# A four-layer attention and Fourier network on one core: head operands packed by halves of the sequence, output-weight pieces chained, stored weight parts loaded one by one

## The chip, the cores and the metric

The kernel runs on one core of a Trainium2 chip. The metric is the device time of one execution in microseconds (us). A core has TensorE (PE; its weight loads are listed as PEld), VectorE (DVE), ScalarE (ACT), GpSimd (POOL) and SyncE (SP), each working through its own list of instructions in order. They wait for each other through semaphores. In this kernel SP issues all transfers between device memory and the on-chip buffer (SBUF); matmul results land in eight banks of a small accumulator memory (PSUM).

## The reference, cut to what matters

The input `x` has 2048 rows (sequence, S) of 640 (D). Four layers follow each other, each with a layer norm before it and the input added after it: attention, Fourier, attention, Fourier, with the same weights both times.

```python
def _A_ref(x, wqkv, wo):
    H = 32; Dh = D // H; W = 256
    qkv = (x @ wqkv).reshape(B, S, 3, H, Dh).transpose(2, 0, 3, 1, 4)
    q, k, v = qkv[0], qkv[1], qkv[2]
    scores = einsum("bhqd,bhkd->bhqk", q, k) * (Dh ** -0.5)
    mask = (idx[:, None] - idx[None, :] >= 0) & (idx[:, None] - idx[None, :] < W)
    p = softmax(where(mask, scores, -1e9), axis=-1)
    o = einsum("bhqk,bhkd->bhqd", p, v)
    return o.transpose(0, 2, 1, 3).reshape(B, S, D) @ wo

def _B_ref(x, dft_seq_re, dft_seq_im, dft_hid_re, dft_hid_im):
    a = einsum("bsd,ed->bse", x, dft_hid_re)
    b = einsum("bsd,ed->bse", x, dft_hid_im)
    return einsum("ts,bse->bte", dft_seq_re, a) - einsum("ts,bse->bte", dft_seq_im, b)

x = x + _A_ref(_layernorm(x), A_wqkv, A_wo)
x = x + _B_ref(_layernorm(x), ...)
x = x + _A_ref(_layernorm(x), A_wqkv, A_wo)
x = x + _B_ref(_layernorm(x), ...)
```

The change touches the attention layers alone: 32 heads of 20 columns, and a window of 256 positions back.

## The kernel before, in words

**Number format.** Every operand of a large product is held as two parts, `hi` (the value rounded to the matmul's format by ACT) and `lo` (what is left, subtracted by DVE or POOL). A product is three matmuls: hi x hi, hi x lo, lo x hi. The output weights `wo`, 640 x 640, are cut into such parts once, in the first attention, and stored in device memory (`wod`) for both.

**The head loop (`heads`, L666).** Heads go in eight quads of four. A quad has 16 blocks of 128 query rows, so there are 128 steps, and `step` runs from -10 to 128. In one step three stages stand beside each other: the scores of block `s = step + 10` (`s_head`, L691), from which DVE takes each row's maximum (L696); the transposed scores of block `t = step` with the maximum subtracted (`t_pair`, L719), their exponentials on ACT (L729) and masks on POOL (L735, L739); and the product with the values of block `v = step - 1` (`pv`, L754), copied by ACT (L761), so that each step has one such copy. Every four blocks (one of the four 512-column blocks of the sequence, `sb`) the maxima are transposed on PE (L704), copied by ACT to `mt` (L707) and sent by SP as a row of the quad's q operand (`qp<-mt`, L709); the transposed scores need that row some four steps after. Every four blocks too, `finish` (L765) sends sums and results out (`sm<-ou`, `o_d<-ou`, `r_d<-rc`), with DVE's reciprocal of the sums between them.

**Operands of a quad (`pack`, L642).** The q and k columns, computed as chunks of 128 rows and stored by 512-column blocks (`qk_d<-c`, 512 KB), are loaded into one of two buffer sets, by quad number odd or even. For each 512-column block there are 12 loads of 20 rows x 2 x 512. The list `due` (L789) says when: for quad q and block j at `s = 16q + 4j - 8`, so a block every four steps; `defer(i // 3, f)` (L862) puts three loads in each of four steps. If a chunk's block isn't yet stored (`packable`), `pack` first runs its pending jobs (`flush`) and advances the slots until it is. Quad 0 is packed before the loop.

**Filling.** Between these stages `fill` gives PE other work, in order: the projections of the later q and k chunks (`project`, L618; L275), then the first three fifths of the output product (`partials`, L1040), then the rest (`late`).

**Slots, lanes, posts.** `tick` (L191) is the clock of the schedule: two slots a step. `post(d, f)` runs `f` d slots later. The lanes "act" and "pool" are queues of small jobs of which each tick emits one. All of this is decided when the program is built; at run time there are only the lists of the engines.

**Pieces of `wo` (`keep_wo`, L548), first attention only.** Ten pieces of 128 x 320: load `rr<-wo` (L557), 5 slots later a cut job (ACT writes `hi`, L237; POOL writes `lo` in two halves of 160 columns, L229), 2 slots later two stores `wo_d<-rr` (L561). A piece starts every six steps, at steps 2, 8, ... 56; at step 62 the three buffers `rr` return to their other use.

**Output product.** `prepare(2)` (L1008), when the projections have two block pairs left, loads the parts of the first three fifths of `wo` (`load_wo`, L1022: two loads of 320 KB for each fifth) and asks for the attention results. The asks wait in `self.asks`; a tick pops one (L196) when three raw buffers of five are free in turn. An ask loads results (`x<-o_d`) and reciprocals (`rr<-r_d`), has POOL scale them and ACT and POOL cut them. `poll_late` (L1097) loads the other two fifths near the end of the loop.

The lines in which the order of the work around the change is set:

```python
                for i, f in enumerate(self.pack(q, j)):
                    defer(i // 3, f)
        if self.asks and self.room(3):
            self.asks.popleft()()
        self.post(5, lambda: self.cut_job("pool", ("wo", i), hi, lo, raw, lambda: self.post(2, keep)))
```

Of the kernel before, what the change touches and what calls it, by code (L numbers as in the profile page):

```python
# [7 lines left out]
F32 = mybir.dt.float32  # L8
# [7 lines left out]
P = 128  # L16
# [51 lines left out]
class Net:  # L68
    def __init__(self, nc, tc, ctx, a):
# [26 lines left out]
        self.od = dram.tile([H, 32, S], F32, name="o_d")  # L96
        self.wod = dram.tile([2, KC, P, D], F32, name="wo_d")
        self.wqd = dram.tile([NCH, P, 2 * D], F32, name="wq_d")
# [92 lines left out]
    def tick(self):  # L191
        self.slot += 1
        for k in sorted(k for k in self.posted if k <= self.slot):
            for f in self.posted.pop(k):
                f()
        if self.asks and self.room(3):  # L196
            self.asks.popleft()()
        for lane in self.lanes.values():
            for _ in range(2 if self.lead else 1):
                if lane and lane[0][0] <= self.slot:  # L200
                    lane.popleft()[2]()
# [18 lines left out]
    def sub_job(self, lane, key, lo, src, hi, done=None):  # L220

        eng = {"dve": self.nc.vector, "pool": self.nc.gpsimd}[lane]
        n = 2 if lane == "pool" and len(src.shape) == 2 else 1
        w = src.shape[-1] // n
# [323 lines left out]
    def keep_wo(self, i):  # L548

        if i == 0:  # L550
            self.wt = [self.slot_tile(f"rr{n}", 512, dt)[:, :320] for n, dt in enumerate((F32R, F32R, F32))]
        if i == 2 * KC:
            self.rr = [self.slot_tile(f"rr{n}", 512, F32) for n in range(3)]
            return
        k, cs = i // 2, slice(i % 2 * 320, i % 2 * 320 + 320)
# [3 lines left out]
        def keep():  # L559
            for n, t in enumerate((hi, lo)):  # L560
                self.nc.sync.dma_start(self.wod[n, k, :, cs], t.bitcast(F32))  # L561
        self.post(5, lambda: self.cut_job("pool", ("wo", i), hi, lo, raw, lambda: self.post(2, keep)))

# [77 lines left out]

    def pack(self, quad, sb):  # L642

        todo = []
        cols = slice(sb * 512, (sb + 1) * 512)
        for c in range(160 * quad // P, -(-160 * (quad + 1) // P)):
            while self.slot is not None and c > 1 and (c, sb) not in self.packable:
                self.flush(("qk", c, sb))
                if self.heavy:
                    self.relieve()  # L650
                self.tick()
# [14 lines left out]
    def heads(self, xsrc, xdst, hook):  # L666
# [120 lines left out]
        for c, u in [(c, u) for c in range(NCH - 2) for u in range(2)] + [(c, sbs[0] // 2) for c, sbs in LAST]:  # L787
            pos[c, u] = 2 * per_piece * (len(pos) + 1)
        due = [(16 * q + 4 * j - AHEAD, pos[-(-160 * (q + 1) // P) - 1, j // 2])  # L789
               for q in range(1, NQ) for j in range(NSB)]  # L790
        self.xsrc = xsrc
# [50 lines left out]
        for step in range(-LEAD, steps + 1):  # L842
# [8 lines left out]
            for f in later.pop(step, []):  # L851
                f()
            if self.fresh and step >= 0 and step % 6 == 2 and step // 6 <= 2 * KC:
                self.keep_wo(step // 6)
            s, t, v = step + LEAD, step, step - 1
            if due and s >= due[0][0]:
                while done[0] < due[0][1]:
                    fill(15)
                due.pop(0)
                q, j = (s + AHEAD) // 16, (s + AHEAD) % 16 // 4  # L860
                for i, f in enumerate(self.pack(q, j)):
                    defer(i // 3, f)  # L862
# [141 lines left out]
    def prepare(self, n):  # L1004
# [3 lines left out]
        if n == 2:  # L1008
# [5 lines left out]
            for k in ks:  # L1014
                self.load_wo(k, self.early_w[k])
            self.ask(0)
# [5 lines left out]
    def load_wo(self, k, w):  # L1022
        for n in range(2):
            self.nc.sync.dma_start(w[n].bitcast(F32), self.wod[n, k])

# [41 lines left out]
    def ready_part(self):  # L1067
        t = self.part_t
        return t == NB or t % 4 or not (self.early_o[t // 4 % 2]["left"])

# [20 lines left out]
    def poll_late(self, n):  # L1091

        if n == 1:
            self.late_w = pairs(cuts(self.qp[0][:, :4 * D], D))
            self.late_c = [self.work.tile([P, 1024], F32, name="cr", tag="c", bufs=3) for _ in range(3)]
            for k in range(EARLY, KC):
                self.load_wo(k, self.late_w[k - EARLY])  # L1097
        if n in (1, 4):
# [801 lines left out]
```

## Time and profile before

| What | us |
|---|---|
| Median of 3 runs (2223.17 to 2227.18) | 2225.28 |
| Time of the profiled execution | 2228.1 |
| Span of the profiled execution, first to last instruction | 2226.4 |
| First head loop, first to last output copy of L761 | 164.7 to 556.6 |
| Second head loop, first to last output copy of L761 | 1274.9 to 1654.4 |

The page shows one profiled execution. Its first part gives the busy time of each engine and its share of the span, then the number of instructions. In views of waits, a row reads "engine, what it was about to do, what ended the wait: us in total, times, longest". In timelines, a row is "start, length, engine, line, operation, output <- inputs (shape) and how many were merged; in brackets the idle time before and what ended it". SPq rows are issues of transfers, whose length is the issue alone; "DMA" rows in the chain of waits run from issue to landing. PE's granted clock is given as a share of full speed.

### The profile page before, as it was taken

Reading aid. Unit: us, or ns where it says so; the run is one execution under the profiler, and the core shown is the slowest. Engines: PE = TensorE matmul, PEld = TensorE weight load, DVE = VectorE, ACT = ScalarE, POOL = GpSimd, SP = SyncE. Lnnn points to the kernel's source line nnn. Section 1 sums busy time; section 2 is a strip of 40 time slices with the busy share of each in tenths; the row PEclk is TensorE's granted clock in tenths of the full one; section 3 lists DMA queues with packets and bytes.
Section 4 is the critical chain, followed back from the end, with each engine's and each line's share of the span. In section 5 each row is a group of like instructions: output and inputs, shape, how many; then the busy total and the mean of one; then the engine's idle time right before and its main releaser. Section 6 shows DMA issues by size and latency. Waiting matters only on the chain.

```text
span 2226.4 us, 48984 instructions
## 1 busy us (share of the span) xinstructions
PE 2127.7 (96%) x17944; PEld 1791.7 (80%) x17944; DVE 1597.3 (72%) x3910; ACT 1115.6 (50%) x2080; POOL 999.4 (45%) x1648
## 2 busy tenths in 40 slices
PE   7999989899989999999999999989889999999999
PEld 7987767677768888889999877767777788888898
DVE  7358777675898768786661578867758978687766
ACT  2127766556554545452441277666565545455332
POOL 3048767776514132332330377668655132331324
PEclk9999999999999999999999999999999999999999
DMA  6556776775635454656645566676844354546653
GB/s 219 176 187 213 219 238 210 209 225 162 195 118 172 137 169 136 224 178 205 207 160 181 170 206 197 215 215 206 233 153 152 117 183 140 173 138 219 218 172 119
DMA packets 227728, 410.14 MB, mean 184 GB/s; under 512 B 40352, under 2 KB 90784, under 8 KB 227488
## 3 DMA queue, kind: packets, MB, share of 16 engines
q1 hardware_dynamic: 227488, 407.01, 57.6%
q8 instruction: 142, 2.33, 0.5%
q14 instruction: 98, 0.80, 0.1%
HBM read 282.13 MB, written 123.60 MB: 182 GB/s over the span
## 4 chain that ended last, share of the span: by engine, by line
PE 76%; DVE 7%; DMA 6%; POOL 3%; ACT 3%; issue 3%; SPq 2%; ACTq 0%; DVEq 0%; POOLq 0%
PE banks L1449 29%; PE banks L257 15%; PE banks L275 12%; PE banks L754 6%; PE banks L719 5%; PE banks L1738 4%; PE banks L691 4%; ACT pt L729 1%; DMA qp<-mt 1%; DMA qp<-qk_d 1%; DVE banks L696 1%; DMA x<-o_d 1%; DMA kp<-qk_d 1%; DVE qp L250 1%; DVE big L1062 1%
## 5 line engine op out<-in xcount | busy, mean ns | idle before, releaser
L696 DVE CUSTOM_DVE_ANT_0 banks<-banks,mask 128x384 f32<-128x384 f32 (+2 forms) x1024 | 528.1, 557 | 164.2 <-PE banks L691 140.1
L729 ACT ACTIVATE pt<-banks 128x768 f32<-128x768 f32 (+2 forms) x512 | 394.2, 771 | 199.0 <-PE banks L719 85.9
L735 POOL TENSOR_SCALAR_AFFINE_SELECT pt<-pt 128x256 f32<-128x256 f32 x512 | 208.9, 408 | 211.4 <-ACT pt L729 194.9
L275 PE MATMUL banks<-big,wc 64*128 64x512 f32 x1920 | 273.3, 397 | 0.4 <-DVE pt L461 0.4
L719 PE MATMUL banks<-qp,kp 61*128 61x384 f32 (+2 forms) x1024 | 210.3, 382 | 33.4 <-DMA qp<-mt 16.5
L691 PE MATMUL banks<-kp,qp 60*128 60x384 f32 (+2 forms) x1024 | 205.8, 345 | 14.3 <-ACT pt L729 10.1
L754 PE MATMUL banks<-pt,vq 128*32 128x128 f32 x5760 | 213.4, 279 | 5.1 <-POOL pt L735 2.8
L275 PEld LDWEIGHTS banks<-big,wc 64*128 64x128 f32 x1920 | 189.5, 187 | 21.9 <-ACT x L594 1.9
L754 PEld LDWEIGHTS banks<-pt,vq 128*32 128x32 f32 x5760 | 143.0, 110 | 55.5 <-issue 37.2
L719 PEld LDWEIGHTS banks<-qp,kp 61*128 61x128 f32 x1024 | 108.6, 185 | 96.4 <-DVE mc L696 56.1
L739 POOL TENSOR_SCALAR_AFFINE_SELECT pt<-pt 128x256 f32<-128x256 f32 x448 | 182.4, 407 | 0.0
L244 ACT ACTIVATE qp<-pt 128x512 fp32r<-128x512 f32 (+1 forms) x195 | 119.8, 624 | 112.9 <-DVE pt L1383 53.5
L244 ACT ACTIVATE c<-pt 128x512 fp32r<-128x512 f32 x150 | 93.6, 626 | 159.1 <-POOL pt L1369 53.0
L250 DVE TENSOR_TENSOR c<-pt,c 128x512 fp32r<-128x512 f32 x150 | 124.1, 828 | 55.5 <-ACT c L244 52.9
L250 DVE TENSOR_TENSOR qp<-pt,qp 128x512 fp32r<-128x512 f32 (+1 forms) x191 | 155.1, 819 | 12.2 <-ACT qp L244 9.5
L1449 PE MATMUL banks<-qp,big 128*128 128x512 f32 x630 | 156.3, 401 | 4.3 <-ACT qp L244 1.8
L1382 POOL TENSOR_TENSOR pt<-pt,pt 128x512 f32<-128x512 f32 x34 | 50.7, 1491 | 239.3 <-DMA pt<-c 153.7
L691 PEld LDWEIGHTS banks<-kp,qp 60*128 60x128 f32 x1024 | 125.2, 188 | 34.7 <-ACT pt L729 13.9
L1449 PEld LDWEIGHTS banks<-qp,big 128*128 128x128 f32 x630 | 121.4, 194 | 31.1 <-ACT qp L244 2.7
L696 DVE DVE_READ_ACCUMULATOR2_ANT mc<- 128x1 f32 x1024 | 145.2, 142 | 0.0
L1449 PE MATMUL banks<-qp,xc 128*128 128x512 f32 x480 | 117.2, 390 | 0.7 <-DVE xc L250 0.7
L1449 PEld LDWEIGHTS banks<-qp,xc 128*128 128x128 f32 x480 | 89.9, 188 | 20.2 <-DVE xc L250 1.6
(242 smaller groups left out, 4442.0 us busy)
## 6 DMA issues: line engine op xcount, KB each, us to landing
pt<-c SPq DMA_DIRECT2D x188, 512.0 KB
qk_d<-c SPq DMA_DIRECT2D x80, 512.0 KB
kp<-qk_d SPq DMA_DIRECT2D x384, 80.0 KB
qp<-qk_d SPq DMA_DIRECT2D x384, 80.0 KB
kp<-u_d SPq DMA_DIRECT2D x32, 640.0 KB
o_d<-ou SPq DMA_DIRECT2D x64, 256.0 KB
x_d<-x SPq DMA_DIRECT2D x48, 320.0 KB
v_d<-pt SPq DMA_DIRECT2D x16, 768.0 KB
```

The lines of the kernel that those rows point to most:

```text
L244: nc.scalar.activation(hi, src, AF.Copy, scale=-1.0 if neg else 1.0)
L250: (eng or nc.vector).tensor_tensor(out=lo, in0=src, in1=hi.bitcast(F32), op=OP.subtract)
L257: self.nc.tensor.matmul(p, x, y, start=n == 0, stop=n == last)
L275: self.nc.tensor.matmul(ps[a], x[r], y[r], start=half + i == 0, stop=half == 1 and i == n - 1, skip_group_check=True)
L691: nc.tensor.matmul(p, qp[quad % 2][b:b + 60, z, qb * P:(qb + 1) * P], kp[quad % 2][b:b + 60, z, k0 * P:(qb + 1) * P], start=True, stop=True)
L696: nc.vector.tensor_tensor_reduce(out=p, in0=p, in1=self.mask[:, 384 - n * P:], scale=1.0, scalar=NEG, op0=OP.add, op1=OP.max, accum_out=mc ...
L719: nc.tensor.matmul(self.banks[:, banks[e], :n * P], kp[quad % 2][b:b + 61, z, kb * P:(kb + 1) * P], qp[quad % 2][b:b + 61, z, kb * P:(kb + ...
L729: nc.scalar.activation(pt[quad, kb][:, 2 * z:2 * z + 2, :n * P], self.banks[:, b0:b1 + 1, :n * P], AF.Exp, scale=SCALE)
L735: nc.gpsimd.affine_select(out=t[:, :, 0:P], in_=t[:, :, 0:P], pattern=[[0, 2], [1, P]], compare_op=OP.is_ge, fill=0.0, base=0, channel_mul ...
L739: nc.gpsimd.affine_select(out=t[:, :, 256:384], in_=t[:, :, 256:384], pattern=[[0, 2], [-1, P]], compare_op=OP.is_gt, fill=0.0, base=0, ch ...
L754: nc.tensor.matmul(self.banks[32 * h:32 * h + 32, bank, :P], vq[:, 96 * (kb % 4) + 21 * h:96 * (kb % 4) + 21 * h + 32], t[:, h, (qb - kb) ...
L1449: nc.tensor.matmul(self.banks[:, bk, :], p, b[q], start=start and m == 0, stop=stop and last and m == 2, skip_group_check=True)
```

## The change

Four things are edited, in the attention alone.

- Quads 1 to 7 are packed by halves of the sequence: 12 loads of 20 rows x 2 x 1024 at `s = 16q - 8` for blocks 0 and 1, and 12 at `s = 16q` for blocks 2 and 3, again three a step. Both blocks of a half have to be stored by then.
- The pieces of `wo` form a chain: piece 0 starts at step -2, and each piece starts the next when its own stores are issued. The cut is posted 9 slots after the load (5 before). POOL subtracts a piece's 320 columns at once. The `rr` buffers return after the last piece.
- `wod` keeps both parts of a fifth side by side, so that one load of 640 KB brings them. At `prepare(2)` these loads are posted 5, 7 and 9 slots later.
- An ask is popped when two raw buffers are free in turn (three before).

```diff
-        self.wod = dram.tile([2, KC, P, D], F32, name="wo_d")
+        self.wod = dram.tile([KC, P, 2, D], F32, name="wo_d")
...
-        if self.asks and self.room(3):
+        if self.asks and self.room(2):
             self.asks.popleft()()
...
-        n = 2 if lane == "pool" and len(src.shape) == 2 else 1
+        n = 2 if lane == "pool" and len(src.shape) == 2 and src.shape[1] > 320 else 1
...
         if i == 0:
             self.wt = [self.slot_tile(f"rr{n}", 512, dt)[:, :320] for n, dt in enumerate((F32R, F32R, F32))]
-        if i == 2 * KC:
-            self.rr = [self.slot_tile(f"rr{n}", 512, F32) for n in range(3)]
-            return
         k, cs = i // 2, slice(i % 2 * 320, i % 2 * 320 + 320)
         hi, lo, raw = self.wt
         self.nc.sync.dma_start(raw, self.a["wo"][:, k, cs])
 
         def keep():
             for n, t in enumerate((hi, lo)):
-                self.nc.sync.dma_start(self.wod[n, k, :, cs], t.bitcast(F32))
-        self.post(5, lambda: self.cut_job("pool", ("wo", i), hi, lo, raw, lambda: self.post(2, keep)))
+                self.nc.sync.dma_start(self.wod[k, :, n, cs], t.bitcast(F32))
+            if i < 2 * KC - 1:
+                self.keep_wo(i + 1)
+            else:
+                self.rr = [self.slot_tile(f"rr{n}", 512, F32) for n in range(3)]
+        self.post(9, lambda: self.cut_job("pool", ("wo", i), hi, lo, raw, lambda: self.post(2, keep)))
...
-    def pack(self, quad, sb):
+    def pack(self, quad, sb, n=1):
 
         todo = []
-        cols = slice(sb * 512, (sb + 1) * 512)
-        for c in range(160 * quad // P, -(-160 * (quad + 1) // P)):
-            while self.slot is not None and c > 1 and (c, sb) not in self.packable:
-                self.flush(("qk", c, sb))
+        cols = slice(sb * 512, (sb + n) * 512)
+        for c, i in [(c, i) for c in range(160 * quad // P, -(-160 * (quad + 1) // P)) for i in range(sb, sb + n)]:
+            while self.slot is not None and c > 1 and (c, i) not in self.packable:
+                self.flush(("qk", c, i))
                 if self.heavy:
                     self.relieve()
                 self.tick()
...
-        due = [(16 * q + 4 * j - AHEAD, pos[-(-160 * (q + 1) // P) - 1, j // 2])
-               for q in range(1, NQ) for j in range(NSB)]
+        due = [(16 * q + 8 * j - AHEAD, pos[-(-160 * (q + 1) // P) - 1, j]) for q in range(1, NQ) for j in range(2)]
...
-            if self.fresh and step >= 0 and step % 6 == 2 and step // 6 <= 2 * KC:
-                self.keep_wo(step // 6)
+            if self.fresh and step == -2:
+                self.keep_wo(0)
...
-                q, j = (s + AHEAD) // 16, (s + AHEAD) % 16 // 4
-                for i, f in enumerate(self.pack(q, j)):
+                q, j = (s + AHEAD) // 16, (s + AHEAD) % 16 // 8
+                for i, f in enumerate(self.pack(q, 2 * j, 2)):
                     defer(i // 3, f)
...
             for k in ks:
-                self.load_wo(k, self.early_w[k])
+                self.post(5 + 2 * k, lambda k=k: self.load_wo(k, self.big[0][:, k * 2 * D:(k + 1) * 2 * D]))
...
     def load_wo(self, k, w):
-        for n in range(2):
-            self.nc.sync.dma_start(w[n].bitcast(F32), self.wod[n, k])
+        self.nc.sync.dma_start(w.bitcast(F32), self.wod[k].rearrange("p l c -> p (l c)"))
...
             for k in range(EARLY, KC):
-                self.load_wo(k, self.late_w[k - EARLY])
+                self.load_wo(k, self.qp[0][:, (k - EARLY) * 2 * D:(k - EARLY + 1) * 2 * D])
```

More of the change, by code (lines that the diff above doesn't have):

```diff
@@ L1068, in ready_part @@
         t = self.part_t
-        return t == NB or t % 4 or not (self.early_o[t // 4 % 2]["left"])
+        return t == NB or t % 4 or not self.early_o[t // 4 % 2]["left"]
     def late_set(self, sb):
```

## Prediction

> **What bounds the kernel now.** I read the page first, then the busy time by stretches, then the waits, then the queue's timeline where PE stood still. The page gives the span and shows TensorE busy nearly throughout, so only its few idle microseconds can be won.
>
> ```profile
> span 2226.4 us, 48984 instructions
> PE 2127.7 (96%) x17944; PEld 1791.7 (80%) x17944; DVE 1597.3 (72%) x3910; ACT 1115.6 (50%) x2080; POOL 999.4 (45%) x1648
> kp<-qk_d SPq DMA_DIRECT2D x384, 80.0 KB
> qk_d<-c SPq DMA_DIRECT2D x80, 512.0 KB
> big<-wo_d SPq DMA_DIRECT2D x12, 320.0 KB
> ```
>
> The change sits in the head loop, which runs twice, and the two passes differ in little but the weight work of the first (`fresh`). Three stretches of each, cut at the same steps (first, 76th and 91st output copy of L761, then the last), give the busy time; after the length come PE, PEld, DVE, ACT, POOL, granted clock, DMA share, GB/s.
>
> ```profile
> 164.70:381.90 217.20, 205.70 (x2879) 156.72 (x2880) 166.08 (x629) 152.89 (x285) 161.92 (x372) 0.98 0.70 218
> 381.90:434.50 52.60, 43.57 (x576) 32.33 (x577) 33.33 (x128) 31.03 (x57) 37.99 (x82) 0.90 0.78 230
> 434.50:556.60 122.10, 111.86 (x1724) 92.43 (x1720) 83.98 (x278) 73.41 (x135) 84.70 (x184) 1.00 0.65 191
> 1274.90:1477.90 203.00, 201.58 (x2879) 154.38 (x2880) 165.42 (x629) 146.63 (x266) 144.52 (x342) 1.00 0.66 203
> 1477.90:1529.30 51.40, 42.84 (x576) 32.01 (x577) 33.41 (x128) 30.99 (x57) 37.86 (x82) 0.93 0.81 230
> 1529.30:1654.40 125.10, 113.76 (x1724) 94.19 (x1720) 83.88 (x279) 73.42 (x136) 84.80 (x184) 0.97 0.63 188
> ```
>
> With the same 2879 matmuls the first stretch takes 217.2 us in the first pass and 203.0 in the second: 14.2 us are lost to the weight work. The second pass shows the undisturbed step: 203.0/75 = 2.71 us, 1.35 a slot. At that pace the 15 steps of the middle stretch are 40.6 us, so it loses about 12 and 11 us. The waits of the first pass and one place of ACT's and SP's timelines tell what the 14.2 are:
>
> ```profile
> ACT rr L237 <- DMA rr<-wo: 5.5, 4, 3.0
> ACT rr L237 <- DMA wo_d<-rr: 4.4, 1, 4.4
> 290.14 0.36 SPq L557 DMA_DIRECT2D rr<-wo  x1
> 294.34 0.47 ACT L237 ACTIVATE rr<-rr 128x320 fp32r<-128x320 f32 x1 [3.00 <-DMA rr<-wo]
> 332.23 0.69 PE L691 MATMUL banks<-kp,qp 60*128 60x384 f32 x1 [4.37 <-ACT pt L729]
> ```
>
> ACT reaches the weight cut before its load has landed and stands with all exponentials queued behind it; PE follows. The middle stretch of the second pass shows the other stall:
>
> ```profile
> 1477.24 2.79 SPq L1024 DMA_DIRECT2D big<-wo_d  x6
> ...
> 1481.84 0.51 SPq L944 DMA_DIRECT2D x<-o_d  x1
> 1482.90 1.87 SPq L654 DMA_DIRECT2D qp<-qk_d  x3
> 1485.44 0.61 SPq L771 DMA_DIRECT2D sm<-ou  x1
> 1486.82 0.34 SPq L772 DMA_DIRECT2D o_d<-ou  x1
> 1487.68 0.43 SPq L777 DMA_DIRECT2D r_d<-rc  x1
> 1489.07 0.37 SPq L573 DMA_DIRECT2D qk_d<-c  x1
> 1490.18 1.06 SPq L654 DMA_DIRECT2D kp<-qk_d  x3
> ...
> 1493.84 1.16 SPq L709 DMA_DIRECT2D qp<-mt  x2
> 1481.84 8.33 DMA x<-o_d
> 1493.84 4.04 DMA qp<-mt
> 1483.60 0.25 ACT L707 ACTIVATE mt<-banks 16x128 fp32r<-16x128 f32 x1
> 1492.09 0.44 PE L691 MATMUL banks<-kp,qp 60*128 60x384 f32 x2 [2.02 <-DVE mc L696]
> 1498.02 0.69 PE L719 MATMUL banks<-qp,kp 61*128 61x384 f32 x2 [5.13 <-DMA qp<-mt]
> ```
>
> All transfers go through SP in order. The load of 1481.84 lands at 1490.17, and the eighth transfer after it goes out at 1490.18: the queue holds eight, and the ninth waits for the oldest. Six weight loads of 320 KB fill it; the row maxima `mt`, ready at 1483.85, go out 10 us later, and PE stands 2.02 and 5.13 us.
>
> **The change part by part.**
>
> *Weight pieces chained, 14.2 us in play.* A piece now starts when the one before is stored, and its cut is posted 9 slots after the load, not 5: 4 x 1.35 = 5.4 us more, over the longest of both waits (3.0, 4.4). From piece store to the next write of `hi` there are ten slots, where the kernel before had four in the worst case. Walking the lanes, the ten pieces end about slot 166, six before `prepare(2)` at 172; no later wait takes the stall's place. POOL does one subtraction of 320 columns for two of 160:
>
> ```profile
> L229 POOL TENSOR_TENSOR rr<-rr,rr x20: 522/527/534, 181.4 to 334.2; 128x160 fp32r<-128x160 f32 x20
> L654 SPq DMA_DIRECT2D kp<-qk_d x384: 273/335/1427, 54.3 to 1592.2; - x192
> ```
>
> That is at most 0.5 us each, on an engine with room: nothing. Bounds of the part: 0 to -14.2; I take -12.7, leaving 1.5 for bursts (below).
>
> *Packing by halves.* Quads 1 to 7 take 24 loads of 160 KB for 48 of 80 KB: 168 issues fewer a pass, x 0.335 = 56 us of SP's time, in a loop of 380 us, and each of these issues also took one of the eight places in the queue. That is why the first pass's queue ran late (the 290.14 load above went out with a cut due at 291). But 12 loads of 160 KB now go in four steps and none in the next four: 1.92 MB in 4 x 2.71 = 10.8 us. With two qk stores of 512 KB, an o store and a v load (1.47 MB) this is 314 GB/s, where the row of the full queue below moved 265. 3.39/0.265 = 12.8 us, 2 us late at the end of the burst, and drained when the next `mt` goes out two slots later. What `mt` may lose shows where nothing is late:
>
> ```profile
> 1440.48 0.25 ACT L707 ACTIVATE mt<-banks 16x128 fp32r<-16x128 f32 x1
> 1447.84 0.44 PE L719 MATMUL banks<-qp,kp 61*128 61x384 f32 x2 [0.35 <-DVE mc L696]
> 1480.00:1500.00 20.00, 12.85 (x170) 9.81 (x163) 11.07 (x41) 8.75 (x18) 9.70 (x21) 0.88 0.91 265
> ```
>
> 7.1 us from copy to use, and a landing takes about 4. In the first pass a burst also meets a 640 KB weight store and 480 KB of pieces: 4.5 MB, 17 us, some 3.5 us late at `mt`: just at the limit. Bounds: 0 to +2 for each of five such bursts; I took 1.5 in all. Loads two blocks early overwrite nothing in use: the blocks of two quads before were last read by step 16(q-2)+7.
>
> *Weight loads spread, room(2).* At `prepare(2)` six loads become three of 640 KB, at 5, 7 and 9 slots. The o loads of block 0 come first, the third two slots earlier, and one of block 1 is let in. Up to the `mt` in question: o 1.28 MB, o of block 1 0.51, one weight load 0.64, qk store 0.51, sums and o store 0.26, three packs 0.48 = 3.69 MB; before, the same count is 4.46 MB and took from 1477.24 to 1497.88, 217 GB/s. Transfers grow from 0.186 to 0.217 MB on average, and with eight in the queue I scale to 254 GB/s: 1.3 + 14.5 us, `mt` at 15.8 to 16.3 against a need at 1483.85 + 7.1 = 13.7 after 1477.24. So 2.5 us late for 7.15 (2.02 + 5.13): -4.65. At 217 it would be 4.6 late, at 265 1.5.
>
> The half clock behind a long gap goes too: the row of 1480 to 1500 has 0.88. [...] Of the 10.8 us that the middle stretch of the second pass loses (51.4 - 40.6), 7.15 and, below, 1.36 are gaps; of the 2.3 left I put 1.5 to this clock: -6.15 a pass, -12.3 in all; bounds -8 to +2 a pass.
>
> *A wait that gets longer.* At step 86 the packing of quad 6 finds chunk 8 not yet stored: it empties the POOL lane ahead of the masks and holds SP until the store has landed. Now it needs blocks 2 and 3, not 2 alone, and the earlier o jobs stand ahead:
>
> ```profile
> 1512.01 1.44 POOL L229 TENSOR_TENSOR c<-x,c 128x256 fp32r<-128x256 f32 x2
> 1515.96 0.41 PE L754 MATMUL banks<-pt,vq 128*32 128x128 f32 x4 [0.37 <-POOL pt L735]
> 1517.37 0.41 PE L754 MATMUL banks<-pt,vq 128*32 128x128 f32 x4 [0.99 <-POOL pt L735]
> 469.04 0.45 PE L719 MATMUL banks<-qp,kp 61*128 61x384 f32 x2 [1.95 <-DMA qp<-mt]
> 1565.32 0.69 PE L719 MATMUL banks<-qp,kp 61*128 61x384 f32 x2 [3.98 <-DMA qp<-mt]
> ```
>
> PE stood 1.36 us. Two more subtractions of 0.72 each and one of an o job come ahead of the masks: +2 a pass (0 to +4), +4 in all. Behind POOL's masks wait the PV matmuls; behind SP's wait stand that step's `mt`, sums and v load, whose 7.1 us are then nearly used up. The additional o load has a second price here: it holds one of the five raw buffers, so the copy of (8, 3) runs the clock of slots on by two at step 83 until one is free, 1.4 us of POOL work sent ahead, on an engine busy 37.86 of 51.4 us; nothing to +1, within the +2.
>
> *The late quads.* The 3.98 us at 1565 (1.95 in the first pass) are again `mt` behind packs, in steps that now have none: -5 in all, clock included; bounds 0 to -8. The four loads at the tail (L1097) become two, not on the path.
>
> Sum: -12.7 - 12.3 + 4 - 5 = -26. The profiled execution took 2228.1 us (span 2226.4), 2.8 above the median 2225.28; 2228.1 - 26 = 2202.1, less 2.8 is 2199.
>
> **The rivals.**
>
> *Only the chain pays.* The middle stretch moves its bytes at 0.81 DMA share already, and the half-pack of quad 6 puts 0.96 MB more into the same steps. From slot 173 to 186 there fall due weights 1.97, o loads 1.79, packs 1.92, qk stores 1.02, o store and v 0.64: 7.3 MB in 18.9 us, 388 GB/s. If the lateness then only moves on to the next `mt`, four steps behind, the spread loads win nothing: -12.7 - 5 + 4 = -13.7, 2212 beside the median. Against it: the stall was one of order, six loads that nobody needed yet ahead of one that PE needed.
>
> *All stalls go.* 14.2 of the first stretch, 2 x 8.65 at `prepare(2)` (7.15 and the clock), 7.5 of the late quads (3.98 and 1.95, and the clock behind the longer), 2 x 1.36 at step 86: 41.7 us, 2184. For it: SP is relieved of 56 us of issues a pass. Against it: step 86 gets more to do, not less.
>
> *Slower: the bursts.* If a burst moves 2 us worse than I reckon, `mt` lands behind its 7.1 us after each one, 14 a pass. It decides from 3 us of lateness in the queue. At 1.5 us each, 28 x 1.5 = 42 less the 26 won: 2241. For it: 314 GB/s wanted, 265 seen when the queue was full. Against it: the first stretches moved 218 and 203 GB/s at shares of 0.70 and 0.66, which is 311 and 308 at full share; at that rate a burst is late by a tenth of a microsecond, and the four steps behind it want no pack at all.
>
> [...]
>
> *It doesn't do what it says.* Fewer issues, yet `mt` and the weight load stand behind the same bytes, since those do not change: 2225. Against it: the 5.4 us that the cut gains are written into the order and depend on no rate.
>
> **How the numbers follow.** Forecast 0.60 (own range 2189 to 2209), only the chain 0.14, all stalls 0.08, slower 0.13, nothing 0.05. Low 2185 to high 2221 leaves out the slower case and part of "all". A measurement here tells 0.2%, 4.5 us: faster 0.82, same 0.05, slower 0.13.
>
> **What would show it.** ACT no longer waits for `rr<-wo` or `wo_d<-rr`, and the first stretch of the first pass is near 204.5; `mt` at the 81st copy goes out within 6 us; three loads of 640 KB stand apart; PE's gaps at step 86 grow to about 3.4. Gaps of L719 for `mt` every eight steps would prove the slower case.

## The result, and the profile after

| Kernel | Median, us | Runs | Ratio to before, 95% interval |
|---|---|---|---|
| before | 2226.23 (2223.17 to 2227.95) | 4 | |
| after | 2260.59 (2254.01 to 2265.38) | 4 | 1.0154 [1.0122, 1.0186] |

The change makes the kernel 34 us slower, where 26 us of gain were forecast. The spans of the profiled executions lie 28.8 us apart. The page of the changed kernel, its span, its busy times and two of the issue rows:

```profile
span 2255.2 us, 48553 instructions
PE 2138.0 (95%) x17944; PEld 1791.5 (79%) x17944; DVE 1594.0 (71%) x3910; ACT 1117.9 (50%) x2080; POOL 1005.7 (45%) x1638
kp<-qk_d SPq DMA_DIRECT2D x168, 160.0 KB
big<-wo_d SPq DMA_DIRECT2D x6, 640.0 KB
```

The change did what it says: 168 loads of 160 KB for 336 of 80 KB in each of the two rows, the same 17944 matmuls. The lines of the head loop have moved by one (the scores are L692, the reciprocal L775, the exponentials L730). The same six stretches as before, cut at the same output copies, with the same columns:

```profile
167.10:389.20 222.10, 208.85 (x2879) 156.60 (x2880) 165.70 (x629) 153.18 (x285) 161.10 (x361) 0.97 0.74 214
389.20:450.60 61.40, 46.19 (x577) 33.88 (x577) 33.30 (x128) 32.34 (x60) 42.95 (x90) 0.86 0.74 198
450.60:577.00 126.40, 114.44 (x1722) 94.01 (x1719) 83.60 (x279) 73.01 (x134) 80.21 (x176) 0.97 0.63 179
1293.50:1496.30 202.80, 200.47 (x2879) 151.96 (x2878) 165.59 (x628) 146.82 (x265) 144.94 (x341) 1.00 0.73 205
1496.30:1557.70 61.40, 46.30 (x576) 33.87 (x577) 33.42 (x128) 32.07 (x59) 42.92 (x90) 0.86 0.73 198
1557.70:1684.50 126.80, 114.73 (x1724) 94.02 (x1720) 83.76 (x279) 73.20 (x134) 80.33 (x177) 0.97 0.65 179
```

Against before, the first stretch of the first pass has +4.9 where -12.7 was forecast; the two middle stretches +8.8 and +10.0; the late ones +4.3 and +1.7. The first stretch of the second pass is unchanged at 202.8, with the same packing but without the weight work of the first pass (the pieces of `wo`, and the cutting and storing of the other weights). So the loss needs either that work beside the packing or the work of the middle stretch.

What PE stands behind has changed too. The page's groups of instructions, each with its idle time and the largest releaser at the end; before, then after:

```profile
L719 PE MATMUL banks<-qp,kp 61*128 61x384 f32 (+2 forms) x1024 | 210.3, 382 | 33.4 <-DMA qp<-mt 16.5
L691 PE MATMUL banks<-kp,qp 60*128 60x384 f32 (+2 forms) x1024 | 205.8, 345 | 14.3 <-ACT pt L729 10.1
```

```profile
L720 PE MATMUL banks<-qp,kp 61*128 61x384 f32 (+2 forms) x1024 | 210.0, 386 | 25.9 <-DVE mc L697 14.1
L692 PE MATMUL banks<-kp,qp 60*128 60x384 f32 (+2 forms) x1024 | 200.2, 350 | 33.9 <-DVE mc L697 32.6
```

The waits for `mt` and for ACT no longer lead (in the first pass `mt` costs 3.6 us for 7.4), and the next scores wait 32.6 us for DVE's row maxima, for 4.1 us before. DVE has no more to do: 1594.0 us busy, for 1597.3. The waits of the first pass say what held it, first of before, then of after:

```profile
DVE rc L774 <- DMA sm<-ou: 4.9, 3, 2.6
```

```profile
DVE rc L775 <- DMA sm<-ou: 33.3, 12, 10.3
PEld banks L692 <- DVE mc L697: 30.5, 27, 7.6
PE banks L692 <- DVE mc L697: 23.1, 10, 7.2
PE banks L720 <- DMA qp<-mt: 3.6, 1, 3.6
```

The reciprocal of the sums (`rc`) stands in DVE's list nine slots after `finish`. In the place shown here `sm` hadn't landed: DVE stood 3.54 us at the reciprocal, the row maxima behind it began at 223.95, as it ended, and PE, whose next scores need the banks that the maxima read, stood 2.95 us. That place in the chain of work that ended last (start, length, what), in the first stretch of the first pass:

```profile
204.78 5.29 DMA kp<-qk_d
...
210.09 0.27 SPq L655
...
210.41 8.42 DMA qp<-qk_d
...
218.89 4.78 DMA sm<-ou
223.67 0.02 issue
223.70 0.25 DVE rc L775
223.95 0.46 DVE banks L697
```

Read it from below. The reciprocal starts as `sm` lands, at 223.67. `sm` went out at 218.89, just after the load of 210.41, eight transfers before it, had landed (210.41 + 8.42 = 218.83). The issue at 210.09, right ahead of that load, had itself waited for the load of 204.78 to land (210.07). A load of 160 KB took 5.29 us early in the burst and 8.42 later. The two engines' own timelines give the price:

```profile
223.70 0.25 DVE L775 RECIPROCAL rc<-sm 128x16 f32<-128x16 f32 x1 [3.54 <-DMA sm<-ou]
```

```profile
224.52 0.44 PE L692 MATMUL banks<-kp,qp 60*128 60x384 f32 x2 [2.95 <-DVE mc L697]
```

The same chain in the middle stretch, where weights and attention results are in the queue as well, ends in the longest `PE banks L692 <- DVE mc` of the waits above, 7.2 us:

```profile
415.74 6.95 DMA sm<-ou
422.69 0.02 issue
422.72 0.25 DVE rc L775
```

Here too `sm` was late before it went out. The output copy that it reads, the 80th, ended at 400.1; nine pack loads, two weight loads, a store and a load of values stood ahead of `sm` in SP's list, and it was issued 15.7 us after that copy.

### The profile page after: what moved, and what is told of

The parts are those of the page before. It is cut to its first block, busy times and chain, and to the rows that moved or that the text cites. A ratio compares the mean times of both kernels' runs of the same rounds, so it can differ in the third digit from the quotient of the medians.

```text
span 2255.2 us, 48553 instructions
## 1 busy us (share of the span) xinstructions
PE 2138.0 (95%) x17944; PEld 1791.5 (79%) x17944; DVE 1594.0 (71%) x3910; ACT 1117.9 (50%) x2080; POOL 1005.7 (45%) x1638
## 4 chain that ended last, share of the span: by engine, by line
PE 71%; DMA 12%; DVE 7%; ACT 3%; POOL 3%; issue 2%; SPq 1%; ACTq 0%; DVEq 0%; POOLq 0%
PE banks L1448 28%; PE banks L257 13%; PE banks L275 10%; PE banks L755 5%; PE banks L1737 5%; PE banks L720 4%; PE banks L692 4%; DMA sm<-ou 3%; DMA qp<-qk_d 3%; DMA rr<-r_d 2%; DMA kp<-u_d 1%; ACT pt L730 1%; DVE banks L697 1%; DMA kp<-qk_d 1%; PE banks L359 1%
## 5 line engine op out<-in xcount | busy, mean ns | idle before, releaser
L730 ACT ACTIVATE pt<-banks 128x768 f32<-128x768 f32 (+2 forms) x512 | 394.9, 772 | 192.2 <-PE banks L720 78.9
L692 PE MATMUL banks<-kp,qp 60*128 60x384 f32 (+2 forms) x1024 | 200.2, 350 | 33.9 <-DVE mc L697 32.6
L692 PEld LDWEIGHTS banks<-kp,qp 60*128 60x128 f32 x1024 | 119.5, 191 | 58.2 <-DVE mc L697 45.3
L250 DVE TENSOR_TENSOR c<-pt,c 128x512 fp32r<-128x512 f32 x150 | 124.3, 830 | 55.2 <-ACT c L244 53.1
L762 ACT ACTIVATE ou<-banks 128x128 f32<-128x128 f32 x256 | 71.3, 279 | 98.6 <-PE banks L755 87.7
```

Source lines behind the costliest of these rows:

```text
L250: (eng or nc.vector).tensor_tensor(out=lo, in0=src, in1=hi.bitcast(F32), op=OP.subtract)
L692: nc.tensor.matmul(p, qp[quad % 2][b:b + 60, z, qb * P:(qb + 1) * P], kp[quad % 2][b:b + 60, z, k0 * P:(qb + 1) * P], start=True, stop=True)
L730: nc.scalar.activation(pt[quad, kb][:, 2 * z:2 * z + 2, :n * P], self.banks[:, b0:b1 + 1, :n * P], AF.Exp, scale=SCALE)
```

## The experiments

Each kernel was compared with before on the same chip. Stage lengths are those of its profiled execution.

### Which part loses

**e1** is before with the packing by halves alone (the hunks of `pack` and `due` in the diff above go with these lines).

```diff
-                q, j = (s + AHEAD) // 16, (s + AHEAD) % 16 // 4
-                for i, f in enumerate(self.pack(q, j)):
+                q, j = (s + AHEAD) // 16, (s + AHEAD) % 16 // 8
+                for i, f in enumerate(self.pack(q, 2 * j, 2)):
```

> The kernel before with the packing by halves alone; pieces, weight loads and asks stay as before. Theory A (the bursts of 160 KB loads run on few engines, the queue of eight falls behind them, the sums sm land late and DVE's reciprocal holds the scores, in both passes and at prepare(2) too): slower than the kernel before by 25 to 45 us, about 2251 to 2271, with DVE rc waiting for sm tens of microseconds. Rival B (the loss of the middle stretches comes from the spread weight loads and the earlier asks): only the first pass's bursts cost, 10 to 20 us, about 2236 to 2246, with the middle stretches near 52.

**e2** is the changed kernel with packing by blocks, the same lines reversed.

> The changed kernel with the packing put back to single blocks of 80 KB loads every four steps; chained pieces, spread weight loads and earlier asks stay. Theory A: faster than the kernel before by 15 to 30 us, about 2196 to 2211, the first stretch of the first pass near 204 and the middle stretches below 50. Rival B: about 2230, the middle stretches near 61 as in the changed kernel.

Measured: e1 2261.74 us, 1.0154 [1.0133, 1.0175]; e2 2232.25, 1.0018 [1.0007, 1.0029]. The packing alone costs as much as the whole change, and the other three edits together win nothing. The middle stretches of e1 take 59.4 and 59.7 us, with the old weight loads and asks, and those of e2 54.7 and 53.0: so the halves lose there, and rival B falls, although its 2230 is near the time of e2. Theory A's 2196 to 2211 for e2 was missed. In the first stretch of the first pass e1 needs 232.6 us, 10.5 more than the changed kernel:

```profile
167.50:400.10 232.60, 211.88 (x2879) 158.69 (x2880) 166.32 (x629) 152.87 (x286) 162.14 (x372) 0.94 0.71 206
```

**e5** is before with the chain alone, **e6** before with the new layout of the weights and the spread loads alone (the hunks of the diff above for each).

> The kernel before with the chained pieces alone (cut nine slots after the load, one POOL subtraction a piece). The step of the prediction: the first stretch of the first pass falls from 217 to about 204.5, all else stays, 2214. Rival: the queue of that stretch is late anyway, so the wait moves from ACT's cut to mt or sm: the first stretch at 210 to 214 and 2220 to 2224.

> The kernel before with the weight loads as three of 640 KB at 5, 7 and 9 slots alone; asks, packs and pieces as before. The step of the prediction: mt at the 81st copy is 2.5 us late for 7.2, middle stretches fall from 52 to about 46, 2214. Rival: the loads now stand in the queue just ahead of that mt and of the sums, and a 640 KB load keeps the queue as long as two of 320 KB: the middle stretches stay at 52 to 55, 2226 to 2232.

Measured: e5 2223.37, 0.9981 [0.9966, 0.9997]; e6 2227.23, 1.0000 [0.998, 1.002]. In e5 ACT no longer waits for `rr`, just as the forecast says, yet the stretch falls by 2.3 us only, to 214.9. The waits of e5 in the first pass show where the stall went:

```profile
PE banks L720 <- DMA qp<-mt: 11.4, 8, 3.8
PE banks L692 <- DVE mc L697: 9.0, 5, 5.8
DVE rc L775 <- DMA sm<-ou: 8.7, 6, 3.1
```

ACT had been standing for a load behind a queue that was late. With ACT out of the way, the next readers of that queue stand for it. With the spread loads it is alike: PE still waits for `mt` in e2, in the first pass for longer than in before:

```profile
398.19 0.69 PE L720 MATMUL banks<-qp,kp 61*128 61x384 f32 x2 [7.68 <-DMA qp<-mt]
```

### Is it the late sums, or the whole queue?

**e3** issues a half's loads two a step, over six steps instead of four. **e4** puts DVE's reciprocal four slots later.

```diff
-                    defer(i // 3, f)
+                    defer(i // 2, f)
```

> The changed kernel with two half-loads issued in a step instead of three, so that a burst lasts six steps and not four; the same loads and bytes. Theory A: it is the rate, so most DVE waits for sm go and the first stretch of the first pass falls from 222 to about 206; 2225 to 2240 in all. If the size of a load and not the rate were what delays the others: unchanged, about 2255 to 2262.

```diff
-            at = (2, 9, 11) if quad < NQ - 1 else (1, 6, 7)
+            at = (2, 13, 15) if quad < NQ - 1 else (1, 6, 7)
```

> The changed kernel with the reciprocal of the sums (and the store behind it) posted four slots later for the first seven quads, so DVE reaches it 5.4 us later; bursts and transfers as they are. Theory A: DVE no longer waits for sm in the steady steps, the first stretch of the first pass falls from 222 to about 205 and the whole to 2235 to 2245. If sm is only the first of several late transfers (mt close behind it): the stalls move to PE L720 for mt, and the time stays within 8 us of 2258.

Measured: e3 2258.95, 1.0150 [1.0118, 1.0181]; e4 2245.00, 1.0081 [1.0056, 1.0106]. In e4 no wait for `sm` is left in the first pass, and 15 us come back, so DVE's wait was on the path. But the first stretch, expected at about 205 us, still takes 220.4; the middle ones fall to 59.8 and 56.0, and the late one of the second pass to 124.3. What takes the place of DVE's wait is the wait that the slower rival had named:

```profile
PE banks L720 <- DMA qp<-mt: 27.1, 8, 5.9
ACT ou L762 <- DMA o_d<-ou: 17.3, 6, 5.8
```

So the whole queue is late behind a burst; `sm` is only the first that somebody waits for. e3 wins nothing: its first stretch takes 221.2 us where about 206 was expected. Its waits for `sm` fall to 8.6 us in the first pass, but its last loads go out two steps nearer to their use, and scores begin to wait for the operands themselves and for what is queued beside them. That this outweighs the relief is how I read these waits; no run isolates it:

```profile
PE banks L720 <- DMA qp<-mt: 9.0, 4, 4.0
DVE rc L775 <- DMA sm<-ou: 8.6, 4, 5.6
PE banks L692 <- DMA vq<-v_d: 7.4, 4, 2.3
PE banks L692 <- DMA qp<-qk_d: 6.6, 4, 2.3
```

**e10** puts the later reciprocal on the kernel with the chain alone.

> The kernel before with the chain of weight pieces and DVE's reciprocal of the sums four slots later (13 for 9; its store 15 for 11), packing by blocks. DVE waited 4.9 us for sm in the first head loop of before. If these waits lay on the path and what follows has room, 2216 to 2221; if the scores wait for mt in their place, 2222 to 2227, as with the chain alone at 2223.

Measured: 2225.43, 0.9997 [0.9981, 1.0012]: without bursts it brings nothing.

**e11** and **e12** have ACT issue `mt` and `sm` itself, in the changed kernel and in before, so that they don't queue on SP.

```diff
-            self.post(at[0], lambda: nc.sync.dma_start(sm, ou[0:P:32, :]))
+            self.post(at[0], lambda: nc.scalar.dma_start(sm, ou[0:P:32, :]))
```

> The changed kernel with the row maxima mt and the sums sm issued by ACT into its own queue instead of SP's; all packs, loads and stores as in the changed kernel. Theory A (these small transfers stand behind the packs' bytes in SP's one list): the DVE waits for sm and the PE waits for mt go, 2220 to 2235. Rival C (the transfer engines themselves are full in a burst, so whatever is needed comes late): the waits move to the operands qp and kp and to the weight cuts, 2245 to 2262.

> The kernel before with mt and sm issued by ACT into its own queue, nothing else. Theory A: the middle stretches lose most of their wait for mt and sm, 52 to about 45 each, and the late quads 5 us: 2206 to 2216. Rival C: within 4 us of the kernel before. If the issues cost ACT as much as they free: 2226 or slower, with the first stretch of the second pass above 204.

Measured: e11 2341.66, 1.0496 [1.045, 1.0541]; e12 2375.27, 1.0658 [1.0629, 1.0687]. Both are far slower, so they say little of the queue: the issues now take time of ACT's own list, as its timeline in e11 shows,

```profile
214.19 0.60 ACTq L772 DMA_DIRECT2D sm<-ou  x1
219.39 1.07 ACTq L710 DMA_DIRECT2D qp<-mt  x2
```

1.7 us every four steps with the next exponentials behind it; by these two rows that is 107 us for the 192 issues of both passes (an estimate, and too high where an issue goes out beside an exponential, as that of 214.19 does). e12 loses 148 us, so this isn't the whole of it. Their waits also show ACT's copies held by the store of the results (`ACT ou L762 <- DMA o_d<-ou`, 27.0 us in the first pass of e11).

### Ten engines, or the bytes of the burst?

The trace of the changed kernel gives the rises of the semaphores: that of each of the 432 loads of 20 rows (`kp<-qk_d`, `qp<-qk_d`) rises once and then ten times, that of each of the 20 stores of 128 rows `wo_d<-rr` sixteen times. Theory A takes the ten for ten of the 16 transfer engines.

**e7** loads 16 rows of 20 from the third quad on, **e8** all 20 rows but 820 columns of 1024; the two bring nearly the same bytes.

```diff
-                    todo.append(lambda d=dst[b:b + 20, :, cols], src=src: put(d, src))
+                    r = 16 if n == 2 and quad > 1 else 20
+                    todo.append(lambda d=dst[b:b + r, :, cols], src=src[:r]: put(d, src))
```

> The changed kernel, but from the third quad on each half load brings 16 of its 20 rows (128 KB; the other four rows keep what an earlier quad left, so the scores are not the reference's; the instructions of all engines are otherwise the same). Theory A, the load of 20 rows runs on ten of sixteen engines and so a burst puts 192 KB on each of ten, and its lateness is what delays the sums sm: with 16 rows each of sixteen engines has 96 KB, the burst is drained in time, DVE's wait for sm goes and the time is 2230 to 2238. Theory B, the number of engines does not matter and a burst is late by its bytes alone: a fifth of the bytes is gone, just as in the next kernel, and both lie together at 2245 to 2252. Theory C, the loss comes from the order or the coarser start of the packing and not from the transfers: 2255 to 2262.

```diff
-                    todo.append(lambda d=dst[b:b + 20, :, cols], src=src: put(d, src))
+                    m = 820 if n == 2 and quad > 1 else 512 * n
+                    d = dst[b:b + 20, :, sb * 512:sb * 512 + m]
+                    todo.append(lambda d=d, src=src[:, :, :m]: put(d, src))
```

> The control to the kernel of 16 rows: all 20 rows, but only 820 of 1024 columns of each half load from the third quad on (131 KB, 2 per cent more than 16 whole rows; the other columns keep what an earlier quad left, so the scores are not the reference's). Theory A, ten engines: 157 KB on each of ten for 192, so most of the loss stays: 2245 to 2255, at least 10 us above the kernel of 16 rows. Theory B, bytes alone: within 3 us of the kernel of 16 rows. Theory C, not the transfers: 2255 to 2262, like the other.

Measured: e7 2231.52, 1.0023 [1.0008, 1.0037]; e8 2218.98, 0.9971 [0.9959, 0.9983]. A fifth fewer bytes takes out most of the loss of the first stretch in either (205.6 and 206.2 us for 222.1), while the middle stretches stay at 57 to 58 us. e8 isn't above e7, as theory A (ten engines) demands, but 12 us below, so theory A falls. Theory B, bytes alone, missed too: it had both at 2245 to 2252 and within 3 us of each other. The same burst in the three kernels, from the first pack load to the last landing, changed kernel, e7 and e8 in turn:

```profile
203.70:222.70 19.00, 17.51 (x243) 12.72 (x234) 14.23 (x52) 14.12 (x28) 13.48 (x31) 1.00 0.78 204
```

```profile
203.30:220.00 16.70, 16.34 (x236) 11.95 (x237) 14.32 (x54) 12.29 (x25) 10.62 (x26) 1.00 0.99 216
```

```profile
205.20:221.80 16.60, 16.25 (x223) 12.07 (x221) 13.80 (x50) 12.78 (x27) 11.33 (x27) 1.00 0.77 212
```

The last two columns show why. With 16 rows the transfer engines are busy at 0.99 instead of 0.77. But they move 216 GB/s for 212: at full share 218 for 275, so at the higher share an engine moves less in its busy time (an estimate). What the ten steps were taken to mean for the time does not hold throughout. An estimate by ten engines for a load of 20 rows and sixteen for all else, each at 265/16 = 16.6 GB/s (the 265 of 1480 to 1500 in before), with the bytes of these stretches, gives 19.0 us for the changed kernel and 16.8 for e8, as measured, but 13.6 for e7, which took 16.7. What sets these 204 to 216 GB/s isn't settled.

**e9** keeps the 160 KB loads of the changed kernel, starts them four steps earlier and spreads them over eight steps.

```diff
-AHEAD = 8
+AHEAD = 12
...
-                    defer(i // 3, f)
+                    defer(2 * i // 3, f)
```

> The changed kernel with the same loads of 160 KB, begun four steps earlier and spread over eight steps and not four, so three loads in two steps: the bytes and engines of before, half the issues, no burst. Theory A, the burst is the loss: DVE's waits for sm fall to a few us in all and the time is that of the kernel with everything but the packing, 2232, within 2225 to 2237. Rival, a single load of 160 KB on ten engines in front of sm or mt is late by itself, or the earlier need of a whole half empties the lanes and fills more: 2240 to 2255.

Measured: 2237.15, 1.0063 [1.0043, 1.0083]. Its first and middle stretch:

```profile
174.00:376.90 202.90, 201.70 (x2887) 153.16 (x2888) 165.29 (x629) 153.22 (x285) 161.43 (x364) 1.00 0.80 233
376.90:437.50 60.60, 45.71 (x600) 34.27 (x600) 33.61 (x127) 32.59 (x59) 45.57 (x93) 0.86 0.82 225
```

The first stretch is as short as the undisturbed 203.0 of before's second pass, at 233 GB/s for the 214 of the changed kernel: not the rate over the stretch was too high, but that over four steps. e9 changes two things, the start and the pace. A slower pace alone, over six steps, didn't do it (e3); a burst begun earlier at the old pace was not run. (Its first copy comes 7 us later than in the changed kernel, since projections are pulled forward; at the 76th copy, 376.9 for 389.2, it is 12.3 ahead.) The middle keeps its whole loss, so the burst is not its cause.

### The middle stretch, and what is left to win

In **e14** and **e16** quads 6 and 7 are packed by blocks as before: e14 has bursts for quads 1 to 5, e16 spreads them as in e9. **e13** is before with the chain and the spread halves of quads 1 to 5, **e15** the same without the chain. The list of e13:

```diff
+        due = sorted([(16 * q + 8 * j - AHEAD - 4, pos[-(-160 * (q + 1) // P) - 1, j], q, 2 * j, 2)
+                      for q in [1, 2, 3, 4, 5] for j in range(2)]
+                     + [(16 * q + 4 * j - AHEAD, pos[-(-160 * (q + 1) // P) - 1, j // 2], q, j, 1)
+                        for q in [6, 7] for j in range(NSB)])
...
+                    defer(n * i // 3, f)
```

> The changed kernel with quads 6 and 7 packed by 512-column blocks as before, quads 1 to 5 by halves in bursts. If the middle stretch's loss comes from halves of quads 6 and 7, it returns to 53 to 55 us in both passes (61.3 and 61.4 now) while the first stretch of the first pass stays near 222: in all 2242 to 2248. If it comes from the spread weight loads and the earlier results, the middle stays near 60 and the time near 2258.

> The changed kernel with quads 1 to 5 packed by halves spread over eight steps (begun four steps earlier) and quads 6 and 7 by blocks. If burst and middle stretch are two causes that add: first stretch of the first pass near 203, middle near 54, in all 2215 to 2223. If the middle keeps its loss whatever the packing does, 2230 to 2238, as with all quads spread.

> The kernel before with two edits: weight pieces chained, and quads 1 to 5 packed by halves spread over eight steps. First stretch of the first pass near 203 (217.2 before), the rest as before: 2210 to 2216. If the stall only moves to another place, 2222 to 2227.

> The kernel before with one edit: quads 1 to 5 packed by halves spread over eight steps, weight pieces every six steps as before. If the fewer issues alone relieve the queue, the waits of ACT for rr go and the first stretch falls to 203 to 207: 2211 to 2218. If the short time from a piece's load to its cut decides (5 slots), ACT still waits and the first stretch stays at 212 to 218: 2221 to 2228.

| Kernel | Median, us | Ratio, 95% interval | First stretch | Middle, both passes |
|---|---|---|---|---|
| e14 | 2236.83 | 1.0043 [1.003, 1.0056] | 223.4 | 53.2, 51.2 |
| e16 | 2222.11 | 0.9974 [0.9959, 0.999] | 202.2 | 49.8, 49.7 |
| e13 | 2209.82 | 0.9910 [0.9884, 0.9937] | 203.8 | 47.2, 47.9 |
| e15 | 2216.55 | 0.9947 [0.9924, 0.997] | 210.0 | 49.8, 47.6 |

e14 against the changed kernel: two quads less by halves bring 24 of the 34 us back, with the middle where it was before and the first stretch still at 223. So burst and middle are two losses. Within the middle, what the halves of quads 6 and 7 do (both blocks of a chunk must be stored first; twelve loads stand beside the weights) wasn't separated further. e13 has the lowest median of the study. Its middle stretches are also shorter than those of before:

```profile
379.60:426.80 47.20, 44.05 (x576) 32.65 (x577) 33.27 (x128) 30.58 (x57) 37.84 (x82) 0.93 0.78 235
1468.50:1516.40 47.90, 42.96 (x575) 31.69 (x577) 33.30 (x128) 30.47 (x57) 37.95 (x82) 0.96 0.74 226
```

Quad 5's last three loads, issued behind the weight loads in before (387.82, behind 381.67), now go out ahead of them, and the gaps for `mt` at the 81st copy (4.6 and 5.1 us of PE in before) shrink to less than 1.6. That is the stall which the spread weight loads were to take out.

**e17** is e13 with quad 1 by blocks, **e18** the same with quads 2 to 5 by blocks too, but begun four steps earlier.

```diff
-                      for q in [2, 3, 4, 5] for j in range(2)]
-                     + [(16 * q + 4 * j - AHEAD, pos[-(-160 * (q + 1) // P) - 1, j // 2], q, j, 1)
+                      for q in [] for j in range(2)]
+                     + [(16 * q + 4 * j - (12 if 1 < q < 6 else AHEAD), pos[-(-160 * (q + 1) // P) - 1, j // 2], q, j, 1)
```

> The kernel before with the chain, and quads 2 to 5 packed by halves spread over eight steps, quad 1 by blocks at its old steps. With quads 1 to 5 the first output copy comes at 175.8 us for 166.6 with the chain alone, with one gap of 5.99 us for mt at 153.55. If that gap is lost time, it goes: 2200 to 2206. If the projections only moved, the time stays at 2207 to 2212.

> The control to the kernel with quads 2 to 5 by halves: the same quads start four steps earlier too, but by blocks, 48 loads of 80 KB a quad. If the earlier start is what helps, within 3 us of the halves. If half the number of issues is what helps, near the chain alone: 2219 to 2225.

Measured: e17 2212.53, 0.9918 [0.9887, 0.9949]; e18 2216.84, 0.9955 [0.994, 0.997]. e17 is no better than e13, so the projections pulled forward cost nothing that can be told; but its four runs range from 2201.93 to 2222.39, too wide to exclude 6 us. The intervals of e18 and e17 overlap. Chain and earlier start together bring about half of e17's gain over before; the chain alone (e5) had 0.9981. Whether fewer issues bring the rest stays open.

## Why the prediction was wrong

**The step that failed** is "packing by halves", priced at "0 to +2 for each of five such bursts; I took 1.5 in all", with the queue "drained when the next `mt` goes out two slots later". Alone it costs 34 us (e1). Three things in it were wrong:

- *The rate.* The burst was drained at 265 GB/s, or 308 and 311 at full share, rates of a queue filled with other transfers. The stretch of the burst moved 204: 3.9 MB in 19.0 us, for which 265 would need 14.6. (The prediction had 12.8 us for 3.39 MB without the pieces, and 17 for 4.5 MB with them and a weight store.)
- *Who is late.* Only `mt` was followed, with its 7.1 us. The load `sm` has a reader too, the reciprocal, and behind that, in DVE's order, the maxima of the next scores: 4.9 us of waits before, 33.3 after. The forecast asked what stands behind `mt` on PE but not what stands behind `sm` on DVE.
- *Where the slack is least.* The middle stretch with quads 6 and 7 was charged +2 a pass for a longer forced wait alone; it lost 8.8 and 10.0 us, and e14 shows that the halves of these quads are the reason.

What was right in that step: "in the first pass a burst also meets" the pieces, "just at the limit". The first stretch loses with the weight work of the first pass and not without it (202.8 in the second pass); the pieces were not taken out alone.

**The chain**, -12.7: the mechanism was right (no wait of ACT for `rr` is left in the first pass) and the size wrong; e5 measures 3.5 us of gain, interval 0.7 to 7.6. The phrase that fails is "no later wait takes the stall's place": `mt` and `sm` take it, since SP's queue was late for all of them. With the queue relieved, e13 is 6.7 us ahead of e15, which lacks the chain; the intervals of the two just overlap.

**The spread weight loads**, -12.3: nothing by e6, and in e2 the gap for `mt` was 7.68 and 5.27 us in the two passes. The count of bytes ahead of `mt` was about right (3.79 MB issued in e2's second pass, for 3.69), the rate of 254 GB/s was not: `mt` landed 17.9 us after the first of these transfers went out, where 15.8 to 16.3 were forecast, which is 212 GB/s by that count. Larger transfers didn't raise the rate here. Counting all bytes moved, before had 255 GB/s from 1477.24 to 1497.88 and e2 241 from 1476.10 to 1494.50. No run shows the 1.5 us a pass that the forecast put to the clock, nor that the shorter gap of 2.5 us would have kept it: in before the granted clock is 0.50 from 396.2 to 406.2, right behind a gap of 2.08 us, and in the changed kernel 0.50 from 226.0 to 229.2, behind the gap of 2.95 us shown above; in before it is 1.00 from 469.0 to 474.0, behind one of 1.95.

**The late quads**, -5: the late stretches became 4.3 and 1.7 us longer. That half of them have no pack did not help; e2, without halves, has 125.4 and 127.7 as well. The halves alone (e1: 125.0 and 123.1), the chain alone (e5: 121.7 and 121.4) and the spread loads alone (e6: 120.3 and 125.4) don't lengthen both, for 122.1 and 125.1 before. Which edit does it wasn't isolated; room(2) was not run alone.

**The longer wait at step 86**, +4: PE's gaps there were 2.28 and 2.03 us for 1.36 before, less than the 3.4 forecast.

**The rivals.** "Slower: the bursts" had the cause and the sign, at a chance of 0.13 and 2241 us. It named `mt`, 14 times a pass; it was `sm` first, and not in the undisturbed stretch of the second pass. Taking `sm` away brings up exactly that wait for `mt` (e4). The evidence held against it, full-share rates of the first stretches, was evidence about other transfers.

## What to carry to other kernels

Grouping transfers into fewer, larger ones saves issues, but if they then go out in a burst, price the burst at the rate of that very transfer in a full queue (here 204 GB/s, where 265 was taken), and follow every small load behind it to its reader and to what stands behind the reader on its engine. Here the late queue shifted its stall from one reader to the next: with no wait for `sm` left, `mt` cost 27.1 us in the first pass (e4), and with none of ACT for `rr`, 11.4 (e5). So removing one wait told little before the queue had room. The packing by halves alone stands at 1.0154 (e1); begun earlier, spread over the whole period and left as it was where the queue is fullest, it stands at 0.9947 (e15), and with the chain beside it at 0.9910 (e13).

## What was not expected of the hardware

- Within the burst shown, a load of 20 rows by 8 KB landed 1.0 to 1.5 us after the one before when several followed each other, and its time from issue to landing grew from 5.29 to 8.42 us within one burst.
- A higher busy share of the transfer engines did not mean more bytes: 0.99 and 216 GB/s with 16 rows (e7), 0.77 and 212 GB/s with 20 (e8). Why e8 is 12 us faster than e7 at the same bytes isn't known. Their profiled executions, 6.0 us apart, differ in the late stretch of the second pass (124.4 and 118.7), not in the bursts.
- Two issues on ACT took 1.07 us and one 0.60 (e11). No work of ACT stands between 219.35 and 220.56, where the two go out; beside the one of 214.19 an exponential ran from 214.11 to 214.93.
